# Tail operands of 128 columns, dilated casts in pieces of 1024 elements, and the last store on ScalarE's queue, in an attention + gated feed-forward kernel

## The chip, the cores and the metric

The kernel runs on one core of a Trainium2 chip. The metric is the device time of one execution in microseconds (us); the median of several executions counts. A core has five engines that run their own instruction streams: TensorE (PE; its weight loads are shown apart as PEld), VectorE (DVE), ScalarE (ACT), GpSimd (POOL) and SyncE (SP). DMA transfers are issued from the streams of SP, POOL or ACT, and all run on the same 16 DMA engines. The profile counts POOL's transfers under queue q0 and those of SP under q1.

## The reference

Inputs are q, k, v of 8 batches x 8 heads x 576 positions x 64, and the weights of a feed-forward part. Heads 0 to 3 look at a plain window of 32 positions back, heads 4 to 7 at every fourth position up to 128 back:

```python
mask_plain = (rel >= 0) & (rel < window)                                  # window = 32
mask_dil = (rel >= 0) & (rel < window * dilation) & (rel % dilation == 0)  # dilation = 4
scores = np.where(masks[None, :, :, :], scale * q @ k.T, -1000000000.0)
attn = softmax(scores)            # over the last axis
x = (attn @ v).transpose(0, 2, 1, 3).reshape(B * S, H * D)    # 4608 x 512
h = x @ w_in                      # 512 -> 2048
out = (h / (1 + exp(-beta * h))) @ w_out                       # 2048 -> 512, fp32
```

## The kernel before

**Two parts in one stream.** The attention of a batch produces 576 columns of xT, the transposed input of the feed-forward part. That part walks over 9 tiles of 512 tokens: for each tile 16 slots of `w_in` (L809, four matmuls of 512 columns, then tanh on ACT, L818, and the gate on DVE, L823) and 4 blocks of `w_out` (L844, sixteen matmuls, an eviction on ACT or DVE, L859 or L861, and a store from SP, L863). A planner (`Plan.run`) simulates all engines with estimated costs and writes every engine's instructions in the order in which it would start them, so that matmuls of the attention stand between those of the feed-forward part. This order is fixed when the program is built, as is the order of each DMA queue.

**Dilated heads.** Their 576 positions are four residues (position mod 4) of 144. In one residue the mask is a plain window of 32, so 128 of the 144 positions make one square of 128 x 128 (scores at L637, values at L712) and the last 16 positions, the *tail*, need the last 48 keys. Tail scores (task T, L607): for each head pair one matmul with `dkt` as stationary operand, 48 keys x 2 residues = 96 columns, and the 64 columns of `qt` moving, into 96 partitions of a bank. The exponential on ACT and a mask multiplication put the result into `ptt` (L574, L578). Tail values (task U, L697): eight matmuls a batch, stationary a slice of `ptt` with 96 rows and 64 columns, moving 65 columns of `vt_`, into 64 partitions. Each of the tasks runs once a batch, eight times in all. The plain heads' scores and values are L671 and L727. L637 and L671 use halves of 64 rows.

**How a batch comes in.** Batches 0 to 2 are loaded directly and transposed on TensorE (L446, L453). For batches 3 to 7, POOL casts q and k from float32 in HBM to bfloat16 in a scratch tensor in HBM, and SP transposes the scratch into SBUF with a DMA (`crossbar`, L436: dk and dq for the dilated heads, kT and qT for the plain ones). POOL's order for a batch is: a tiny `pace` copy (L921) that waits for the xT of the batch two earlier, the dilated cast of k, that of q, the plain cast of k, loads of v (st, two vt), the plain cast of q, another load of v (vp). A dilated cast is a copy of one contiguous stretch of 147,456 elements; the program before cuts it into 16 rows of 9216 elements. A plain cast moves runs of 64 elements.

**How a batch goes out.** From batch 2 on, normalized values go to a scratch tensor x in HBM (`back_dma`: x<-xsp L473, x<-xdm L481, x<-xdt L486) and SP transposes them into xT (L500). All of these, the crossbars of a later batch and the output stores stand in one queue order of SP: what waits there holds up everything issued behind it.

**The end.** The last block of 128 tokens is cut into columns 0 to 256, 256 to 384 and 384 to 512, each with its eviction and its store.

Of the kernel before, what the change touches and what calls it, by code (L numbers as in the profile page):

```python
# [9 lines left out]
BF16 = mybir.dt.bfloat16  # L10
ACT = mybir.ActivationFunctionType
# [163 lines left out]
def kernel(  # L175
# [19 lines left out]
    C = 4  # L195
    CT = S // C
    UT = CT - P
    KTL = UT + WIN
# [23 lines left out]
    const = lambda shape, dt, name: const_pool.tile(shape, dt, name=name)  # L222
    BANKS = [psum_pool.tile([P, 512], FP32, name=f"bank{i}") for i in range(8)]
    plan = Plan(range(8))
    E = {"ACT": nc.scalar, "DVE": nc.vector, "POOL": nc.gpsimd}

    def bank(g, dt=FP32):
        b = BANKS[g.bank][:]
        return b if dt == FP32 else b.bitcast(BF16)

    def copy(e, out, in_):
        (nc.scalar.copy if e == "ACT" else E[e].tensor_copy)(out=out, in_=in_)  # L232
# [21 lines left out]
    rcp = [const([P, 3, 2], FP32, f"rcp{i}") for i in range(8)]  # L254
    pt = [const([P, NI * 2, P], BF16, f"pt{x}") for x in range(2)]
    ptd = const([P, 2, 2, 4, P], BF16, "ptd")
    ptt = const([P, 2, 272], BF16, "ptt")
    ptt_own = ptt[0:2 * KTL, :, 0:256].rearrange("p c (m s) -> p c m s", s=2 * UT)[:, :, :, 0:UT]
    ptt_of = lambda c, h4: ptt[0:2 * KTL].rearrange("p c m -> p (c m)")[
        :, 256 * c + 64 * h4:256 * c + 64 * h4 + 64]  # L260
    xsp = [const([QT, 3, 2, 2, D], BF16, f"xsp{j}") for j in range(2)]
    xdm = const([P, C, 2, 2, D], BF16, "xdm")
    xdt = const([C * UT, 2, 2, D], BF16, "xdt")
# [9 lines left out]
    qt = [const([P, 2, 2, 4, UT], BF16, f"qt{i}") for i in range(2)]  # L273
    dk = [const([P, 2, 4, CT], BF16, f"dk{i}") for i in range(2)]
    dq = [const([P, 2, 4, CT], BF16, f"dq{i}") for i in range(2)]
    dkt = [const([P, 4, KTL, 2], BF16, f"dkt{i}") for i in range(2)]
    vp = [const([P, 4 * NI, DV], BF16, f"vp{i}") for i in range(2)]
    vd = [const([P, 4, C, DV], BF16, f"vd{i}") for i in range(2)]
    vt_ = [const([2 * KTL, 2, 4, DV], BF16, f"vt{i}") for i in range(2)]
# [3 lines left out]
    mm = lambda n: n / 2.4 + 2.5  # L283
# [16 lines left out]
    def t_fill1(e):  # L300
        for x in range(2):
            nc.vector.memset(kT[x][:, :, 0:WIN], 0.0)
            nc.vector.memset(qt[x][:], 0.0)
    fill1 = plan.op([("DVE", 300)], t_fill1, vt=-8)

    def t_fill2(e):
# [112 lines left out]
    def cast(b, z, h0, deps, vt):  # L419

        dst = scratch[b, z, h0] = dram_pool.tile([S * 4 * D], BF16, name=f"s{b}_{z}_{h0}")
        src = (k, q)[z][b, h0:h0 + 4]
        if h0:
            args = (dst[:].rearrange("(a e) -> a e", e=1024), src.rearrange("h s d -> (h s d)").rearrange("(a e) -> a e", e=1024))
        else:
            args = (dst[:].rearrange("(s h d) -> s h d", h=4, d=D), src.rearrange("h s d -> s h d"))
        return load("POOL", args, deps, vt, 576, .38 if h0 else .2, 500 if h0 else 1700)
# [76 lines left out]
    def attention(b, ld, names, vts):  # L504
# [3 lines left out]
        kv = b % 2  # L508
        if b < DIRECT:
            for n in [x for x in names if x[0] in "KQ"]:  # L510
                z, kind, i = "KQ".index(n[0]), n[1], int(n[2])
                vt = vt_of[n]
                g = Group("a")
                src = ld["qk", z, 0 if kind == "P" else 4]
                tr = plan.op([("PE", (18 * mm(64) if kind == "P" else 6 * mm(QT)))],
                             lambda e, g=g, z=z, kind=kind, i=i: t_transposes(g, z, kind, i),
# [15 lines left out]


        def mixed(e):
            copy(e, dkt[kv][:], dk[kv][:, :, :, CT - KTL:].rearrange("p r h k -> p h k r"))
        o = plan.op([("DVE", 450), ("POOL", 550)], mixed,
                    (steps["KD0"] + steps["KD1"] if b < DIRECT else ready["D"][0:1]) + war(("dkt", kv)), vt_of["T"] - .01, sbuf=True)
        used(("dk", kv, 0), o)
# [60 lines left out]
        for name in [n for n in names if n[0] in "ST"]:  # L599
            vt = vt_of[name]  # L600
            if name == "T":
                g = Group("s")

                def score(e, g=g):
                    sc = bank(g)[0:2 * KTL, 0:256].rearrange("p (c h r u) -> p h c r u", h=4, c=2, r=2)
                    for h4 in range(4):
                        nc.tensor.matmul(sc[:, h4], lhsT=dkt[kv][:, h4].rearrange("p k r -> p (k r)"),  # L607
                                         rhs=qt[kv][:, :, :, h4], start=True, stop=True)
                deps = tail_ready
                sop = plan.op([("PE", 4 * mm(64))], score,  # L610
                              deps, vt, acquire=g)
                used(("dkt", kv), sop)
                used(("qt", kv), sop)
                exp_and_mask(("T",), sop, g, vt, 256,
                             lambda g=g: bank(g)[0:2 * KTL, 0:256].rearrange("p (c m u) -> p c m u", c=2, u=UT),
                             lambda: ptt_own,
                             lambda: mask_t[0:2 * KTL].rearrange("p c h r u -> p c (h r) u"), [("pt", "T")])
                continue
            x = int(name[1])
# [69 lines left out]
        for name in [n for n in names if n[0] in "VU"]:  # L689
            vt = vt_of[name]  # L690
            g = Group("a")
            if name == "U":
                def values(e, g=g):
                    pv = bank(g)[0:C * UT, 0:4 * (D + 1)].rearrange("p (h e) -> p h e", h=4)
                    for h4 in range(4):
                        for c in range(2):
                            nc.tensor.matmul(pv[:, h4], lhsT=ptt_of(c, h4), rhs=vt_[kv][:, c, h4, 0:D + 1],  # L697
                                             start=(c == 0), stop=(c == 1))
                vop = plan.op([("PE", 8 * mm(D + 1))], values, [sdone["T",]] + vdeps["T"], vt, acquire=g)
                used(("vt", kv), vop)  # L700
                used(("pt", "T"), vop)
                normed("U", vop, g, vt, C * UT, 4,
                       lambda g=g: bank(g)[0:C * UT, 0:4 * (D + 1)].rearrange("p (h e) -> p h e", h=4),
                       xdt[:].rearrange("p x h d -> p (x h) d"), "xdt")
                continue
            x, j = int(name[1]), int(name[2])
            if x >= 2:
                def values(e, x=x, j=j, g=g):
                    pv = bank(g)[:, 0:4 * (D + 1)].rearrange("p (r h e) -> p r h e", r=2, h=2)
                    for r in range(2):  # L710
                        for a in range(2):
                            nc.tensor.matmul(pv[:, r, a], lhsT=ptd[:, x - 2, j, 2 * r + a],  # L712
                                             rhs=vd[kv][:, 2 * (x - 2) + a, 2 * r + j, 0:D + 1],
                                             start=True, stop=True)
                vop = plan.op([("PE", 4 * mm(D + 1))], values, [sdone[x, j]] + vdeps["D"], vt, acquire=g)
                used(("vd", kv), vop)
                used(("pt", x, j), vop)
                normed((x, j), vop, g, vt, P, 4,
                       lambda g=g: bank(g)[:, 0:4 * (D + 1)].rearrange("p (r h e) -> p r h e", r=2, h=2),
                       xdm[:].rearrange("p (r c) x h d -> p c r x h d", c=2)[:, j, :, x - 2], "xdm")  # L720
                continue

            def values(e, x=x, j=j, g=g):
                pv = bank(g)[:, 0:6 * (D + 1)].rearrange("p (m h e) -> p m h e", m=3, h=2)
                for a in range(3):
                    for h2 in range(2):
                        nc.tensor.matmul(pv[:, a, h2, :], lhsT=pt[x][:, (3 * j + a) * 2 + h2],  # L727
                                         rhs=vp[kv][:, (2 * x + h2) * NI + 3 * j + a, 0:D + 1],
                                         start=True, stop=True)
            vop = plan.op([("PE", 6 * mm(D + 1))], values,  # L730
                          [sdone[x, j, 0], sdone[x, j, 1]]
                          + vdeps["P", x], vt, acquire=g)
            used(("vp", kv), vop)
            for i in range(3 * j, 3 * j + 3):
                used(("pt", x, i), vop)
            normed((x, j), vop, g, vt, QT, 6,
                   lambda g=g: bank(g)[0:QT, 0:6 * (D + 1)].rearrange("p (m h e) -> p m h e", m=3, h=2),
                   xsp[j][:, :, x], ("xs", x, j))
# [3 lines left out]
        for name in [n for n in names if n[0] in "XY" and b < BY_DMA]:  # L742
            vt = vt_of[name]
            x = int(name[1])
            g = Group("a")
# [86 lines left out]
    def block(t, tb, vts):  # L832
        last_one = (t, tb) == (NTT - 1, 3)
        cuts = (0, HD // 2, 3 * HD // 4, HD) if last_one else (0, HD)
        for i, (lo, hi) in enumerate(zip(cuts, cuts[1:])):
            block_cols(t, tb, [x + i for x in vts], lo, hi)

    def block_cols(t, tb, vts, lo, hi):
        g = Group("z" if t == NTT - 1 else "o")
        prev = None  # L840
        for part in range(4):
# [15 lines left out]
        def evac(e):  # L857
            if e == "ACT":
                nc.scalar.mul(out=ob[:, lo:hi], in_=bank(g)[:, lo:hi], mul=0.5)  # L859
            else:  # L860
                nc.vector.tensor_single_scalar(out=ob[:, lo:hi], in_=bank(g)[:, lo:hi], scalar=0.5, op=ALU.mult)  # L861
        ev = plan.op([act(hi - lo), dve(hi - lo)], evac, [prev] + w, vts[3] - .01, group=g)
        so = plan.op([("SP", 400)], lambda e: nc.sync.dma_start(out=out[r0:r0 + P, lo:hi], in_=ob[:, lo:hi]),  # L863
                     [ev], vts[3], dma=.5 * (hi - lo) * 1000 / 350)
        used(key, so)

# [122 lines left out]
```

The softmax here doesn't subtract the row's maximum and nothing guards it: scores larger than these inputs give would overflow.

## Time and profile before

| what | value |
|---|---|
| device time, median of 5 executions | 308.0 us (307.39, 307.79, 308.0, 308.46, 309.72) |
| the profiled execution: own time / span from first to last instruction | 309.72 us / 308.0 us |
| TensorE clock granted | full in all 40 slices |
| L844 matmuls, 512 columns wide x560 | 140.6 us busy, 379 ns each with the drain |
| L809 matmuls, 512 columns wide x568 | 139.6 us busy, 379 ns each with the drain |
| L697 matmuls x64 / L607 matmuls x32 | 3.7 us, 198 ns each / 2.7 us, 206 ns each |
| DMA, mean 138 GB/s | 42.47 MB in 116,096 packets |
| q0 (POOL) / q1 (SP), share of the 16 engines' span | 62.6% / 37.0% |
| casts s<-in_k, s<-in_q, issue to landing, median | 7.4 us / 10.6 us |

Engines overlap, so busy times do not add up to the span. A matmul's shown duration includes its drain, which overlaps the next one; four matmuls of 512 columns stand 0.86 us apart from the next four. In an order of time, "[2.07 <-DMA x]" is idle time of the engine before that row and what ended it. In rows on DMA queues the columns are packets, MB written, and the packets' time as a share of 16 engines over the stretch asked for; packets of both queues can be under way in one engine at once, so that a share may pass 100%.

### The profile page before, as it was taken

What the parts mean: (1) busy time and instruction counts of PE and PEld (TensorE: products, weight loads), DVE (VectorE), ACT (ScalarE), POOL (GpSimd) and SP (SyncE); (2) the same over time, 40 slices, a digit from 0 to 9 for tenths busy, and PEclk for the clock granted to TensorE, in tenths of its full rate; (3) what the DMA queues carried; (4) which work ended last, traced back from release to release, by engine and by line L of the source; (5) the groups of instructions that cost most, each with busy time, mean ns of one, the idle gap of its engine ahead of it and who ended that gap; (6) DMA issues with size and microseconds to landing.
All of it is one profiled execution on the core that took longest, in us unless ns stands there. A gap on an engine that the chain in (4) does not pass through costs nothing.

```text
span 308.0 us, 6034 instructions
## 1 busy us (share of the span) xinstructions
PE 298.2 (97%) x2312; PEld 150.1 (49%) x2312; DVE 182.4 (59%) x420; ACT 170.8 (55%) x315; POOL 89.7 (29%) x132
## 2 busy tenths in 40 slices
PE   7899999999999979999999999999999999999995
PEld 5564545654544435445444444444444444444454
DVE  3578864988867645875677567756763434344300
ACT  2666963977447543765565556555555444455411
POOL 8987562845063106310641072200000000000000
PEclk9999999999999999999999999999999999999999
DMA  6999999999899999999899989995233100010122
GB/s 96 174 210 203 206 182 213 187 144 185 177 193 173 157 182 159 157 161 215 160 154 179 187 165 152 164 150 155 84 99 75 38 34 34 34 36 34 49 85 72
DMA packets 116096, 42.47 MB, mean 138 GB/s; under 512 B 93748, under 2 KB 110916, under 8 KB 115908
## 3 DMA queue, kind: packets, MB, share of 16 engines
q0 software_dynamic: 65392, 19.66, 62.6%
q1 hardware_dynamic: 50676, 22.43, 37.0%
q8 instruction: 18, 0.29, 0.4%
q14 instruction: 10, 0.08, 0.1%
HBM read 39.32 MB, written 18.87 MB: 189 GB/s over the span
## 4 chain that ended last, share of the span: by engine, by line
PE 74%; DMA 17%; DVE 4%; issue 1%; POOL 1%; SPq 1%; ACT 1%; POOLq 0%; ACTq 0%; DVEq 0%
PE bank L844 33%; PE bank L809 33%; DMA vd<-in_v_dram 4%; DMA st<-in_v_dram 4%; DMA xT<-x 3%; DMA dq<-s 3%; DMA st<-in_q_dram 2%; DVE g L823 2%; PE bank L727 1%; DMA x<-xsp 1%; PE bank L671 1%; PE bank L453 1%; PE bank L637 1%; PE bank L712 1%; PE bank L697 1%
## 5 line engine op out<-in xcount | busy, mean ns | idle before, releaser
L844 PE MATMUL bank<-w_out_bf,g 128*128 128x512 bf16 (+2 forms) x608 | 143.6, 368 | 0.0
L823 DVE SCALAR_TENSOR_TENSOR g<-tnh,bank 128x512 bf16<-128x512 bf16 x144 | 97.7, 684 | 75.0 <-ACT tnh L818 74.3
L809 PE MATMUL bank<-xT,w_in_bf 128*128 128x512 bf16 (+1 forms) x584 | 141.4, 376 | 0.5 <-DMA xT<-x 0.5
L818 ACT ACTIVATE tnh<-bank,beta_half 128x512 bf16<-128x512 f32 x144 | 98.5, 689 | 75.9 <-PE bank L809 74.8
L809 PEld LDWEIGHTS <-w_in_bf 128*128 128x128 bf16 x584 | 54.6, 98 | 60.8 <-DMA xT<-x 0.9
L844 PEld LDWEIGHTS <-g 128*128 128x128 bf16 x608 | 54.7, 98 | 55.8
L859 ACT ACTIVATE osb<-bank 128x512 f32<-128x512 f32 (+1 forms) x36 | 21.2, 589 | 32.2 <-PE bank L844 32.1
L574 ACT ACTIVATE pt<-bank 128x288 bf16<-128x288 f32 x64 | 21.6, 422 | 5.8 <-PE bank L671 5.8
L574 ACT ACTIVATE ptd<-bank 128x512 bf16<-128x512 f32 x32 | 16.9, 607 | 7.4 <-PE bank L637 7.4
L594 DVE TENSOR_TENSOR xsp<-bank,rcp 96x384 bf16<-96x384 f32 x32 | 17.7, 554 | 1.1
L382 POOL DMA_DIRECT2D vp<-in_v_dram x10 | 18.0, 1804 | 0.5 <-PE bank L453 0.5
L593 DVE RECIPROCAL rcp<-bank 128x4 f32<-128x4 f32 (+2 forms) x72 | 12.9, 179 | 6.8 <-PE bank L727 4.8
L578 DVE TENSOR_TENSOR ptd<-ptd,mask_d 128x512 bf16<-128x512 bf16 x27 | 11.9, 452 | 5.7 <-ACT ptd L574 4.5
L594 DVE TENSOR_TENSOR xdm<-bank,rcp 128x256 bf16<-128x256 f32 x32 | 13.6, 424 | 1.1
L382 POOL DMA_DIRECT2D vt<-in_v_dram x16 | 13.7, 1038 | 0.0
L382 POOL DMA_DIRECT2D s<-in_q_dram x10 | 13.6, 1356 | 0.0
L921 POOL COPY pace<-xT 1x2 bf16<-1x2 bf16 x4 | 0.7, 176 | 42.8 <-DMA xT<-x 35.7
L727 PEld LDWEIGHTS <-pt 128*128 128x128 bf16 x192 | 9.4, 97 | 5.9
L382 POOL DMA_DIRECT2D s<-in_k_dram x10 | 11.0, 1104 | 1.2 <-issue 1.2
L232 POOL COPY vd<-st 128x1024 bf16<-128x1024 bf16 x4 | 4.1, 1036 | 22.7 <-DMA st<-in_v_dram 22.7
L232 POOL COPY dkt<-dk 128x384 bf16<-128x384 bf16 x7 | 3.8, 541 | 23.8 <-DMA dk<-s 18.2
L727 PE MATMUL bank<-vp,pt 128*128 128x65 bf16 x192 | 10.4, 193 | 0.0
(107 smaller groups left out, 181.9 us busy)
## 6 DMA issues: line engine op xcount, KB each, us to landing
out_dram<-osb SPq DMA_DIRECT2D x35, 256.0 KB, 2.8
s<-in_k_dram POOLq DMA_DIRECT2D x10, 288.0 KB, 7.4
s<-in_q_dram POOLq DMA_DIRECT2D x10, 288.0 KB, 10.6
vp<-in_v_dram POOLq DMA_DIRECT2D x7, 384.0 KB, 18.5
w_out_bf<-in_moe_w_out_dram POOLq DMA_DIRECT2D x2, 1024.0 KB, 16.8
st<-in_k_dram POOLq DMA_DIRECT2D x6, 288.0 KB, 14.0
st<-in_q_dram POOLq DMA_DIRECT2D x6, 288.0 KB, 12.9
x<-xsp SPq DMA_DIRECT2D x12, 144.0 KB, 8.3
```

Source lines behind the costliest of these rows:

```text
L232: (nc.scalar.copy if e == "ACT" else E[e].tensor_copy)(out=out, in_=in_)
L382: {"POOL": nc.gpsimd, "SP": nc.sync}[queue].dma_start(out=out, in_=in_)
L574: nc.scalar.activation(out=w(), in_=sc(), func=ACT.Exp, scale=SCALE)
L578: E[e].tensor_tensor(out=w(), in0=w(), in1=m(), op=ALU.mult)
L593: nc.vector.reciprocal(out=r, in_=p[..., D])
L594: nc.vector.tensor_tensor(out=dst, in0=p[..., 0:D], in1=r.unsqueeze(len(p.shape) - 1).to_broadcast(list(p.shape[:-1]) + [D]), op=ALU.mult)
L727: nc.tensor.matmul(pv[:, a, h2, :], lhsT=pt[x][:, (3 * j + a) * 2 + h2], rhs=vp[kv][:, (2 * x + h2) * NI + 3 * j + a, 0:D + 1], start=True ...
L809: nc.tensor.matmul(bank(g)[:, a:z], lhsT=w_in_bf[:, kt, fb * P:(fb + 1) * P], rhs=xT[:, kt, xo + a:xo + z], start=(i == 0 and kt == kts[0] ...
L818: nc.scalar.activation(out=th[:, 0:n], in_=bank(g)[:, 0:n], func=ACT.Tanh, scale=beta_half[:, fb:fb + 1])
L823: nc.vector.scalar_tensor_tensor(out=g_t[t % 2][:, fb, c0:c0 + n], in0=th[:, 0:n], scalar=1.0, in1=bank(g)[:, 0:n], op0=ALU.add, op1=ALU.mult)
L844: nc.tensor.matmul(bank(g)[:, lo:hi], lhsT=g_t[t % 2][:, fb, tb * P:(tb + 1) * P], rhs=w_out_bf[:, fb, lo:hi], start=(fb == 0), stop=(fb = ...
L859: nc.scalar.mul(out=ob[:, lo:hi], in_=bank(g)[:, lo:hi], mul=0.5)
```

## The change

Three edits:

- **Tail.** `dkt` gets 32 more columns, zeroed at the start, and each tail score matmul takes 128 stationary columns from the start of its head's 96, so that the last 32 are those of the next head (or the zeros). It writes all 128 partitions of the bank; the exponential reads the first 96 as before. `ptt` is laid out flat with 32 more columns, and each tail value matmul takes 128 stationary columns instead of 64, the later 64 of the next slice; its result fills 128 partitions, of which the first 64 are read as before. The planner's cost of a tail score matmul goes from that of 64 columns to that of 68.
- **Dilated casts.** The same elements are copied in a view of 16 x 9 x 1024: the outer index takes every sixteenth piece of 1024 elements, and each outer entry has 9 such pieces, which are not contiguous.
- **Last store.** The store of the last 128 columns is issued from ACT instead of SP.

The order of the instructions on every engine is the same as before but for three points: DVE has two more memsets at the start, SP loses its last store, and ACT has it at its end.

```diff
-    ptt = const([P, 2, 272], BF16, "ptt")
-    ptt_own = ptt[0:2 * KTL, :, 0:256].rearrange("p c (m s) -> p c m s", s=2 * UT)[:, :, :, 0:UT]
-    ptt_of = lambda c, h4: ptt[0:2 * KTL].rearrange("p c m -> p (c m)")[
-        :, 256 * c + 64 * h4:256 * c + 64 * h4 + 64]
+    ptt = const([P, 2 * 272 + 32], BF16, "ptt")
+    ptt_own = ptt[0:2 * KTL, 0:2 * 272].rearrange("p (c m) -> p c m", c=2)[:, :, 0:256].rearrange(
+        "p c (m s) -> p c m s", s=2 * UT)[:, :, :, 0:UT]
+    ptt_of = lambda c, h4: ptt[0:2 * KTL, 256 * c + 64 * h4:256 * c + 64 * h4 + P]
...
-    dkt = [const([P, 4, KTL, 2], BF16, f"dkt{i}") for i in range(2)]
+    dkt_all = [const([P, 4 * 2 * KTL + 32], BF16, f"dkt{i}") for i in range(2)]
+    dkt = [d[:, 0:4 * 2 * KTL].rearrange("p (h k r) -> p h k r", h=4, r=2) for d in dkt_all]
...
             nc.vector.memset(qt[x][:], 0.0)
+            nc.vector.memset(dkt_all[x][:, 4 * 2 * KTL:], 0.0)
...
         if h0:
-            args = (dst[:].rearrange("(a e) -> a e", e=1024), src.rearrange("h s d -> (h s d)").rearrange("(a e) -> a e", e=1024))
+            args = [x.rearrange("(a c e) -> c a e", c=16, e=1024) for x in (dst[:], src.rearrange("h s d -> (h s d)"))]
...
-                    sc = bank(g)[0:2 * KTL, 0:256].rearrange("p (c h r u) -> p h c r u", h=4, c=2, r=2)
+                    sc = bank(g)[:, 0:256].rearrange("p (c h r u) -> p h c r u", h=4, c=2, r=2)
                     for h4 in range(4):
-                        nc.tensor.matmul(sc[:, h4], lhsT=dkt[kv][:, h4].rearrange("p k r -> p (k r)"),
+                        nc.tensor.matmul(sc[:, h4], lhsT=dkt_all[kv][:, 2 * KTL * h4:2 * KTL * h4 + P],
                                          rhs=qt[kv][:, :, :, h4], start=True, stop=True)
-                sop = plan.op([("PE", 4 * mm(64))], score,
+                sop = plan.op([("PE", 4 * mm(68))], score,
...
                 def values(e, g=g):
-                    pv = bank(g)[0:C * UT, 0:4 * (D + 1)].rearrange("p (h e) -> p h e", h=4)
+                    pv = bank(g)[:, 0:4 * (D + 1)].rearrange("p (h e) -> p h e", h=4)
...
-        so = plan.op([("SP", 400)], lambda e: nc.sync.dma_start(out=out[r0:r0 + P, lo:hi], in_=ob[:, lo:hi]),
+        so = plan.op([("ACT" if last_one and hi == HD else "SP", 400)],
+                     lambda e: (nc.scalar if e == "ACT" else nc.sync).dma_start(out=out[r0:r0 + P, lo:hi], in_=ob[:, lo:hi]),
                      [ev], vts[3], dma=.5 * (hi - lo) * 1000 / 350)
```

More of the change, by code (lines that the diff above doesn't have):

```diff
@@ L534, in mixed @@
         def mixed(e):
-            copy(e, dkt[kv][:], dk[kv][:, :, :, CT - KTL:].rearrange("p r h k -> p h k r"))
+            copy(e, dkt[kv], dk[kv][:, :, :, CT - KTL:].rearrange("p r h k -> p h k r"))
         o = plan.op([("DVE", 450), ("POOL", 550)], mixed,
@@ L835, in block, with block_cols @@
         for i, (lo, hi) in enumerate(zip(cuts, cuts[1:])):
-            block_cols(t, tb, [x + i for x in vts], lo, hi)
-    def block_cols(t, tb, vts, lo, hi):
+            block_cols(t, tb, [x + i for x in vts], lo, hi, last_one)
+    def block_cols(t, tb, vts, lo, hi, last_one):
         g = Group("z" if t == NTT - 1 else "o")
```

## The prediction

> **What bounds the kernel now.** I read the page first, then the groups of TensorE by shape, then its waits and its order of time, then the order of time of SP's queue, last the DMA queues in short windows. The page says that TensorE is the bound and that its own work leaves few holes:
>
> ```profile
> PE 298.2 (97%) x2312; PEld 150.1 (49%) x2312; DVE 182.4 (59%) x420; ACT 170.8 (55%) x315; POOL 89.7 (29%) x132
> PE 74%; DMA 17%; DVE 4%; issue 1%; POOL 1%; SPq 1%; ACT 1%; POOLq 0%; ACTq 0%; DVEq 0%
> ```
>
> 308.0 - 298.2 = 9.8 us are idle: some 4 before 45 us (first loads), 3.3 after the last matmul, and two waits for a transfer between. So two things shorten the time: TensorE's own work after 45 us, and those waits. This is TensorE's order of time at them, and around the tail of one batch:
>
> ```profile
> 112.18 0.62 PE L637 MATMUL bank<-dq,dk 64*128 64x128 bf16 x16 [2.07 <-DMA dq<-s]
> 113.61 0.33 PE L607 MATMUL bank<-qt,dkt 128*96 128x64 bf16 x4
> 113.77 1.03 PE L844 MATMUL bank<-w_out_bf,g 128*128 128x512 bf16 x4
> 114.63 0.28 PE L712 MATMUL bank<-vd,ptd 128*128 128x65 bf16 x4
> 114.76 1.03 PE L844 MATMUL bank<-w_out_bf,g 128*128 128x512 bf16 x4
> 115.62 0.41 PE L712 MATMUL bank<-vd,ptd 128*128 128x65 bf16 x8
> 115.86 1.02 PE L844 MATMUL bank<-w_out_bf,g 128*128 128x512 bf16 x4
> 116.73 0.29 PE L712 MATMUL bank<-vd,ptd 128*128 128x65 bf16 x4
> 116.94 0.44 PE L697 MATMUL bank<-vt,ptt 96*64 96x65 bf16 x8
> 117.31 1.04 PE L844 MATMUL bank<-w_out_bf,g 128*128 128x512 bf16 x4
> 209.79 1.47 PE L809 MATMUL bank<-xT,w_in_bf 128*128 128x512 bf16 x6 [0.45 <-DMA xT<-x]
> ```
>
> Columns: start, duration with the drain, then the work. What a group costs TensorE is the distance from its start to the next one's.
>
> **Part 1, the tail's wider stationary operands.** Nothing is added on TensorE: the same matmuls stream the same 64 or 65 columns and only the stationary side is wider. Tail values (L697, 8 matmuls): 117.31 - 116.94 = 0.37 us, where eight full-width L712 with the same 65 columns take 115.86 - 115.62 = 0.24. Entering them costs too: four L712 take 0.13 us (114.76 - 114.63) ahead of L844, but 0.21 (116.94 - 116.73) ahead of L697. So a tail costs 0.13 + 0.08 = 0.21 us more than full-width matmuls would. Tail scores (L607, 4 matmuls): 113.77 - 113.61 = 0.16 against 0.13, so 0.03. That 96 rows stay (L697) should not matter: L446 has 96*128 and shows neither an entry nor an exit cost, about 43 ns each for 96 columns.
>
> Behind the first 45 us there are seven L697 groups (at 49, 66, 83, 117, 147, 178 and 214 us) and six L607 groups (61, 80, 114, 144, 175, 206): 7 x 0.21 + 6 x 0.03 = 1.65 us; 3 x 0.21 + 2 x 0.03 = 0.69 of it lies ahead of the wait at 109.7 to 112.2, 0.96 behind. The earlier tails lie between waits for first loads and give nothing. Lower end nil (the width isn't the cause), upper end 2 us with the early ones. I take 1.65. It costs DVE two short memsets (the 128x16 ones took 65 to 85 ns) and a longer one in the first microseconds, where DVE waits for loads; on the path they would be 0.2 us.
>
> The Trainium skill has two rules here that disagree. "TensorE: Matmul & The Clock Gate", section "LDWEIGHTS (loading the stationary operand)", has the load take columns / 1.2 ns: 53 ns for 64 columns, 107 for 128, which speaks against the change; if all of it showed, 64 loads would lose 3.4 us and 32 loads from 80 to 107 ns another 0.9. Its section "Weight-path perf modes" has a fast load that needs all 128 columns. The rows side with the second:
>
> ```profile
> L697 PEld LDWEIGHTS <-ptt 96*64 96x64 bf16 x64 | 2.7, 110 | 1.7 <-DMA vt<-in_v_dram 0.8 <-issue 0.6
> L607 PEld LDWEIGHTS <-dkt 128*96 128x96 bf16 x32 | 2.5, 124 | 1.4
> L712 PEld LDWEIGHTS <-ptd 128*128 128x128 bf16 x128 | 6.7, 98 | 4.7 <-issue 0.2
> ```
>
> A full 128-column load takes 98 ns, one of 96 columns 124, one of 64 columns 110.
>
> **Part 2, the casts in pieces.** Each of batches 3 to 7 issues two dilated casts from POOL at its start. SP's queue while batch 4 is fetched:
>
> ```profile
> 88.56 0.63 SPq L473 DMA_DIRECT2D x<-xsp  x1
> 92.45 0.34 SPq L863 DMA_DIRECT2D out_dram<-osb  x1
> 97.92 1.52 SPq L500 DMA_TRANSPOSE xT<-x  x1
> 99.62 4.46 SPq L436 DMA_TRANSPOSE dk<-s  x1
> 104.14 2.72 SPq L436 DMA_TRANSPOSE dq<-s  x1
> ```
>
> SP waits from 92.8 to 97.9 for the x<-xsp issued at 88.56; all behind it (dk, then dq, which ends TensorE's 2.07 us) waits too. The casts were complete at 94.89 and 96.46, so SP was held by the store, not by them. Why 9.3 us, where the one issued at 77.51 took 4.2? The DMA queues from 119.5 to 121.5 us, 88.5 to 91 (two lines) and 102.5 to 106.5 (two lines):
>
> ```profile
> q0 software_dynamic: 16, 0.29, 123.9%
> ...
> q0 software_dynamic: 15, 0.28, 89.9%
> q1 hardware_dynamic: 57, 0.03, 4.7%
> ...
> q1 hardware_dynamic: 1679, 0.42, 81.6%
> q0 software_dynamic: 1630, 0.21, 78.9%
> ```
>
> A cast is 16 packets of 18 KB, one an engine, 1.4 to 3 us each; while they run SP's queue (q1) moves nearly nothing. With small packets in both queues they alternate one for one (1679 and 1630). In 2 KB pieces, 9 an engine and cast, SP's packets go between them. Ahead of and in x<-xsp stand 8 packets an engine of an output store (256 KB in 2 KB packets) and 18 of its own (288 rows of 512 B). The price of a piece is in no row for a copy from HBM to HBM. Nearest below: from 18.6 to 22.6 us q0 alone wrote 0.84 MB (505 packets, most of them 2 KB pieces of w_in), 210 GB/s, so the 0.59 MB of two casts take 2.8 us. Above: today's 0.59 MB from 119.5 to 124.8, 5.3 us. I take 4 us, 0.22 a piece. From 88.7, eight pieces pass with the output store (8 x (0.22 + 0.09) = 2.5, to 91.2), ten with x<-xsp (10 x (0.22 + 0.03) = 2.5, to 93.7), then eight of its packets against 32 ns ones (0.5, to 94.2), and some 0.8 us from last packet to landing as now: 95.0. SP goes on 2.9 us earlier, the casts land by then too (1.5 to 2 us earlier), and dq lands at 112.0 - 2.9 = 109.1, where TensorE wants it at 109.9 - 0.7 = 109.2. So the wait of 2.07 us just goes, and the 0.69 from ahead of it is kept. Ends: all 2.07 and no more; or nothing, when the pieces do not let q1 through.
>
> Against it speaks the Trainium skill, "DMA: Bandwidth & Descriptors", section "Queues, rings and completion order": an engine drains a whole packet, typically 9 to 17 descriptors, of one ring before it switches. If nine pieces are one such packet, nothing is won here; another section of the page, "SWDGE vs HWDGE vs iDMA", prefers packets of at most 4096 B, which is one or two pieces.
>
> Costs: each cast now has 144 rows instead of 16; POOL's issue took 0.51 to 0.57 us, loads of 192 to 256 rows (st) 0.64 to 0.78, so up to 0.25 each, 0.5 a batch ahead of the next issues on POOL. That is hidden: the plain cast issued at 88.49 sends its first packet at 93.5, behind the dilated ones in the ring. Uncovered, it is 0.5 us on the plain q cast, for which SP waits (196.9 to 202.2) before qT and the xT that TensorE awaits at 209.79. That wait of 0.45 I leave in: TensorE comes earlier, and so does the DMA side (casts of batch 5 wait for the xT of batch 3, behind the same SP queue). In batches 5 to 7 dq landed 5 to 6.7 us before L637 asked, so nothing more is to be gained there.
>
> **Part 3, the last store.** DVE ends the last eviction at 305.02; SP, busy until 305.19 with the store before, issues at 305.28 and sees it land at 306.90. ACT is free from 304.83, so it issues some 0.2 us earlier; SP's closing waits follow. Ends: a gain of 0.3, or a loss of 1 if a queue never used before starts slowly (stores from SP took 1.6 us at least and 2.7 at the median from issue to landing; no row shows one from ACT). Nothing stands behind it on ACT. I take -0.2.
>
> **Sum.** 1.65 + 2.07 + 0.2 = 3.9 us off the profiled execution's 309.72 (span 308.0 and 1.72 around it): 305.8. Of the runs shown it is the slowest, 1.7 over the median 308.0; TensorE's clock is full throughout, so what differs is probably waits, and I credit the median with two thirds of the 2.07 (1.4): 308.0 - 1.65 - 1.4 - 0.2 = 304.7.
>
> **Rivals.**
> *The casts' pieces free nothing* (0.20). For it: nothing shows how the two rings mix at 2 KB. The wait stays and swallows the 0.69; the wait at 209.79 swallows up to 0.75 of the 0.96, so 0.2 to 0.96 + 0.2: 306.8 to 307.6, say 307.2.
> *The width is not what L697 pays for* (0.06). The entry cost would then stay because of its 96 rows; L446 speaks against. 308.0 - 1.4 - 0.2 = 306.4.
> *The pieces slow the casting queue* (0.13). Place: q0's ring, each piece now waiting for a q1 packet; the plain q cast of batch 7 lands after 202.2 - (what TensorE gains), SP issues qT and xT late, and L809 at 209.79 has no slack. Price: at 0.33 us a piece (3 us, the longest packet, over 9) two casts take 6 us and the mixing adds 1, so 1.7 more a batch; three batches (5 to 7) follow one another through POOL's pace copy, 5.1 in all, less 1.65 + 0.2 gained: 311; with one or two batches passing it on 309 to 310. I give it 309.8. It decides from a slip of 0.7 us a batch. Against it: SP's backlog of 290 to 600 packets, now drained after the casts at the cost of the plain ones, goes in their shadow.
>
> **Numbers.** Forecast 304.7 (0.61), own range 302.9 to 306.2. An 8-in-10 range takes in most of the first rival: 302.9 to 308.0. What this kernel's runs can tell from no change is about 0.5%, 1.5 us: faster is under 306.5, slower over 309.5. Faster 0.59 of the forecast's, 0.04 of the width's, 0.05 of the first rival's: 0.68; slower 0.11, from the third; same 0.21.
>
> **What would show it.** L697 with 128 columns: eight in 0.24 us, loads of 98 ns, no 0.08 ahead of them. Right after the casts start, q1 with hundreds of packets where it has 57; x<-xsp of batch 2 landed by about 95, dq issued before 102, L637 of batch 4 without a wait, or one under 0.7. Wrong if the wait at L637 stays at 2 us, if SP's wait for the plain casts (202.2) or L809's 0.45 grow beyond 1 us, or if the last store lands over 1.7 us after its issue.

## The result and the profile after

| kernel | median of its executions, us | lowest to highest | ratio to before, 95% interval |
|---|---|---|---|
| before | 307.68 (56 executions, the five of the table above among them) | 306.41 to 310.85 | |
| after | 305.76 (30 executions) | 304.98 to 307.2 | 0.994 (0.9927 to 0.9953) |

The change saves 1.9 us, 0.6%; the interval of the ratio is 1.45 to 2.25 us of 307.68. The forecast was a gain of 3.3. The profiled execution of after took 306.6 us with a span of 304.9, 3.1 us less than the one shown of before. That is more than the medians differ, so the two traces cannot simply be subtracted. What of it is the change, and what is one execution against another, is the main question below.

This is the page of after: span, busy times, the two DMA queues, ACT's new queue q10 (packets, MB, share of the 16 engines) and the chain by engine:

```profile
span 304.9 us, 6036 instructions
PE 296.5 (97%) x2312; PEld 149.1 (49%) x2312; DVE 182.1 (60%) x422; ACT 170.9 (56%) x315; POOL 90.3 (30%) x132
q0 software_dynamic: 66672, 19.66, 63.7%
q1 hardware_dynamic: 50532, 22.36, 36.5%
q10 hardware_dynamic: 144, 0.07, 0.1%
PE 72%; DMA 18%; DVE 4%; ACT 2%; issue 1%; POOL 1%; SPq 1%; POOLq 0%; ACTq 0%; DVEq 0%
```

TensorE is still the bound and has 1.7 us less to do (298.2 before). The DMA share of the chain did not fall. TensorE's order of time in after, at the wait for batch 4 and around the next tail, answers to the rows of before:

```profile
110.96 0.62 PE L639 MATMUL bank<-dq,dk 64*128 64x128 bf16 x16 [1.43 <-DMA dq<-s]
...
112.39 0.28 PE L609 MATMUL bank<-qt,dkt 128*128 128x64 bf16 x4
112.50 1.03 PE L846 MATMUL bank<-w_out_bf,g 128*128 128x512 bf16 x4
...
114.36 0.41 PE L714 MATMUL bank<-vd,ptd 128*128 128x65 bf16 x8
114.60 1.02 PE L846 MATMUL bank<-w_out_bf,g 128*128 128x512 bf16 x4
115.46 0.28 PE L714 MATMUL bank<-vd,ptd 128*128 128x65 bf16 x4
115.58 0.41 PE L699 MATMUL bank<-vt,ptt 96*128 96x65 bf16 x8
115.83 1.03 PE L846 MATMUL bank<-w_out_bf,g 128*128 128x512 bf16 x4
```

The lines stand two or three further down than in before: L639 was L637, L609 was L607, L699 was L697, L714 was L712, L846 was L844, and the store L866 was L863. Below, a line is called by its number in the kernel it is read in.

The tail now costs what full-width matmuls cost. From start to start, eight tail values take 115.83 - 115.58 = 0.25 us (0.37 before), the four L714 ahead of them 0.12 (0.21 before), four tail scores 112.50 - 112.39 = 0.11 (0.16 before). That is 0.21 and 0.05 a batch. The weight loads show it as well (groups by shape; the pair is busy time and mean ns of one):

```profile
L699 PEld LDWEIGHTS <-ptt 96*128 96x128 bf16 x64 | 2.6, 97 | 1.4 <-DMA vt<-in_v_dram 1.0 <-issue 0.2
L609 PEld LDWEIGHTS <-dkt 128*128 128x128 bf16 x32 | 1.9, 98 | 1.5
```

They fell from 110 and 124 ns to 97 and 98, although L699 still has 96 rows.

But the wait at L639 is there: 1.43 us where 2.07 stood and nothing to 0.7 was forecast. SP's order of time in after, over the same stretch as before:

```profile
88.55 1.69 SPq L475 DMA_DIRECT2D x<-xsp  x1
91.88 0.34 SPq L866 DMA_DIRECT2D out_dram<-osb  x1
96.12 1.56 SPq L502 DMA_TRANSPOSE xT<-x  x1
97.86 4.12 SPq L438 DMA_TRANSPOSE dk<-s  x1
102.03 2.82 SPq L438 DMA_TRANSPOSE dq<-s  x1
```

SP goes on at 96.12 instead of 97.92 and issues dq at 102.03 instead of 104.14. So SP's store gets through sooner, though not by the 2.9 us forecast. Of these 2.1 us at the issue only 1.2 are left at the landing: dq landed at 110.82 in after and at 112.04 in before. The DMA queues show SP's packets passing in the five microseconds from 88.5, first in before, then in after (packets, MB, share of the 16 engines):

```profile
q0 software_dynamic: 46, 0.57, 84.7%
q1 hardware_dynamic: 152, 0.21, 12.3%
```

```profile
q0 software_dynamic: 254, 0.49, 73.7%
q1 hardware_dynamic: 264, 0.32, 20.5%
```

Where the pieces meet the output store that stands ahead of x<-xsp, they pass one for one. In after, from 90.25 to 91.5 us:

```profile
q0 software_dynamic: 75, 0.15, 73.9%
q1 hardware_dynamic: 75, 0.15, 36.2%
```

Last the end, DVE's last eviction and the store issued from ACT, in order of time:

```profile
301.77 0.29 DVE L863 TENSOR_SCALAR osb<-bank 128x128 f32<-128x128 f32 x1 [1.30 <-PE bank L846]
302.15 0.38 ACTq L866 DMA_DIRECT2D out_dram<-osb  x1
```

The issue comes 0.09 us after the eviction's end (0.26 before), and the store lands at 303.77, 1.62 us after its issue.

### The profile page after: what moved, and what is told of

Same layout as the page of the kernel before. It is cut to its first block, busy times and chain, and to the rows that moved or that the text cites. A ratio compares the mean times of both kernels' runs of the same rounds, so it can differ in the third digit from the quotient of the medians.

```text
span 304.9 us, 6036 instructions
## 1 busy us (share of the span) xinstructions
PE 296.5 (97%) x2312; PEld 149.1 (49%) x2312; DVE 182.1 (60%) x422; ACT 170.9 (56%) x315; POOL 90.3 (30%) x132
## 4 chain that ended last, share of the span: by engine, by line
PE 72%; DMA 18%; DVE 4%; ACT 2%; issue 1%; POOL 1%; SPq 1%; POOLq 0%; ACTq 0%; DVEq 0%
PE bank L846 33%; PE bank L811 32%; DMA vd<-in_v_dram 4%; DMA st<-in_q_dram 4%; DMA st<-in_v_dram 3%; DMA dq<-s 3%; DVE g L825 2%; DMA st<-in_k_dram 2%; DMA x<-xsp 2%; DMA xT<-x 1%; PE bank L729 1%; PE bank L673 1%; PE bank L639 1%; PE bank L714 1%; ACT ptd L576 1%
## 5 line engine op out<-in xcount | busy, mean ns | idle before, releaser
L846 PE MATMUL bank<-w_out_bf,g 128*128 128x512 bf16 (+2 forms) x608 | 143.3, 368 | 0.0
L846 PEld LDWEIGHTS <-g 128*128 128x128 bf16 x608 | 54.6, 98 | 55.7
L576 ACT ACTIVATE ptd<-bank 128x512 bf16<-128x512 f32 x32 | 16.9, 603 | 6.8 <-PE bank L639 6.7
L232 POOL COPY vd<-st 128x1024 bf16<-128x1024 bf16 x4 | 4.1, 1036 | 16.3 <-DMA st<-in_v_dram 16.3
## 6 DMA issues: line engine op xcount, KB each, us to landing
w_out_bf<-in_moe_w_out_dram POOLq DMA_DIRECT2D x2, 1024.0 KB, 16.7
```

What stands on the lines that cost most here:

```text
L576: nc.scalar.activation(out=w(), in_=sc(), func=ACT.Exp, scale=SCALE)
L846: nc.tensor.matmul(bank(g)[:, lo:hi], lhsT=g_t[t % 2][:, fb, tb * P:(tb + 1) * P], rhs=w_out_bf[:, fb, lo:hi], start=(fb == 0), stop=(fb = ...
```

## The experiments

Theory: SP's store, held up behind large cast packets, was what made dq late, and pieces cure it. Rival: the DMA engines are full from the casts until dq lands, so that the order of the packets hardly matters, only their number. Where a table says "cast to dq", it is the time from the issue of batch 4's dilated k cast to the landing of its dq, in the one profiled execution. Each kernel is compared with executions of before measured beside it, through the ratio; it is formed from the executions and is not exactly the quotient of the two medians.

### One part at a time

Tail alone: the kernel before with the tail edit, without these two:

```diff
-            args = [x.rearrange("(a c e) -> c a e", c=16, e=1024) for x in (dst[:], src.rearrange("h s d -> (h s d)"))]
+            args = (dst[:].rearrange("(a e) -> a e", e=1024), src.rearrange("h s d -> (h s d)").rearrange("(a e) -> a e", e=1024))
...
-        so = plan.op([("ACT" if last_one and hi == HD else "SP", 400)],
+        so = plan.op([("SP", 400)],
```

> The kernel before with the tail's edit alone. Waits theory (the wait of L637 for dq of batch 4 and that of L809 for xT swallow what TensorE gains ahead of them): the eight L697 take 0.24 us and four L607 0.12, yet of the 1.65 us only the part behind the waits stays, 0.2 to 1.1 us: 306.6 to 307.5 against 307.7; the wait at L637 grows to 2.5 to 2.9 us in the profile. Rival (in most executions these waits are short, so TensorE's work is the bound): the whole 1.65 stays, 306.0.

The casts alone, with the first of these two lines as in after and the other edits undone:

> The kernel before with the dilated casts in pieces alone. Waits theory: x<-xsp of batch 2 lands 1.5 to 2.5 us earlier after the casts' start, dq of batch 4 lands 1 to 2 us earlier, L637 waits 0.5 to 1.2 us in place of 2.07 and the 0.45 of L809 goes: 306.2 to 306.9 against 307.7. Rival (the waits are short in most executions): no change within 0.3 us.

The store alone, with only the second line as in after:

> The kernel before with the last store on ACT's queue alone. Both theories: issue 0.1 to 0.2 us after DVE's last eviction and landing 1.6 us later, 0.15 to 0.2 us less from the last matmul to the end: 307.5. Rival: the closing waits of SP end at the same time, 307.7.

| kernel | median, us | before beside it | ratio, 95% | cast to dq, us | wait for dq, us |
|---|---|---|---|---|---|
| tail alone | 306.0 | 307.49 | 0.994 (0.9912 to 0.9968) | 24.61 | 1.77 |
| casts alone | 306.89 | 307.49 | 0.9972 (0.9944 to 0.9999) | 23.85 | 0.39 |
| last store alone | 307.36 | 307.49 | 0.9989 (0.9962 to 1.0016) | 24.60 | 2.08 |

The tail alone has the ratio of the whole change. Its order of time, with the wait and the group of tail values:

```profile
110.61 0.62 PE L639 MATMUL bank<-dq,dk 64*128 64x128 bf16 x16 [1.77 <-DMA dq<-s]
...
115.23 0.41 PE L699 MATMUL bank<-vt,ptt 96*128 96x65 bf16 x8
115.47 1.03 PE L846 MATMUL bank<-w_out_bf,g 128*128 128x512 bf16 x4
```

The wait stays near its old length and yet the kernel is 1.5 us faster by the medians, 1.8 by the ratio (1.0 to 2.7). What the waits theory expected the waits to take back of the tail's gain (a wait of 2.5 to 2.9 us and 306.6 to 307.5), they did not take back; the number that came is its rival's, 306.0.

The casts alone bring 0.2% to 0.3%, at the limit of what can be told. The last store alone cannot be told from nothing in the time, but the trace shows it:

```profile
306.53 0.29 DVE L861 TENSOR_SCALAR osb<-bank 128x128 f32<-128x128 f32 x1 [1.30 <-PE bank L844]
306.90 0.38 ACTq L864 DMA_DIRECT2D out_dram<-osb  x1
```

The issue again stands 0.08 us behind the eviction, and from the start of the last matmul to the end of the span it takes 3.37 us, as in after, where before and the tail alone have 3.54 and 3.53. So 0.17 us. (TensorE ran at half rate from 114 to 117 us in this profiled execution, mean granted clock 0.993, so its span of 309.6 is not used.)

### Another execution of before

> The kernel before, looked at once more. Corrected theory: its wait at L637 differs from one execution to the next with the start of batch 4's casts; 1.4 to 2.3 us, cast to dq 23.5 to 24.7. Rival (it is nearly always 2.07): 1.9 to 2.2 and 24.5 to 24.7.

Another profiled execution of before took 306.61 us with a span of 304.9. TensorE's order of time:

```profile
106.79 2.75 PE L844 MATMUL bank<-w_out_bf,g 128*128 128x512 bf16 x12
109.47 0.62 PE L637 MATMUL bank<-dq,dk 64*128 64x128 bf16 x16
```

No wait stands between these rows. The 2.07 us on which the forecast rested 1.4 of its 3.3 belong to the slow end of before's executions: cast to dq took 23.22 us here and 24.61 there. Both the expectation (a wait of 1.4 to 2.3 us) and its rival missed. The wait for xT of 0.45 us at 209.79 is missing here, too, so that its absence from after's trace is not to be put down to the change. Nor are SP's clock times. Its order of time here, with the old rows:

```profile
96.36 1.87 SPq L500 DMA_TRANSPOSE xT<-x  x1
98.41 3.93 SPq L436 DMA_TRANSPOSE dk<-s  x1
102.38 2.72 SPq L436 DMA_TRANSPOSE dq<-s  x1
```

These are nearly the times of after (96.12 and 102.03), because the casts were issued at 86.06 us here, at 87.43 in the first execution and at 87.80 in after. Only times counted from the casts can be compared: SP goes on 10.5 and 10.3 us after them in the two executions of before, 8.3 in after.

With two executions of before, the span can be cut at the wait, at the start of the matmuls that need dq of batch 4:

| execution | span | start of L637/L639 | from there to the end |
|---|---|---|---|
| before, first | 308.0 | 112.18 | 195.8 (with the 0.45 wait for xT) |
| before, second | 304.9 | 109.47 | 195.4 |
| casts alone | 304.5 | 109.31 | 195.2 |
| tail alone | 304.7 | 110.61 | 194.1 |
| after | 304.9 | 110.96 | 193.9 |

The right column scatters little and shows the change: 195.2 to 194.1 is the tail's width (1.1 us; four batches at 0.21 + 0.05 make 1.04) and 194.1 to 193.9 the store. Executions that differ in the casts alone are still up to 0.2 us apart here (195.4 and 195.2) without a wait that the traces show. The middle column scatters by 2.7 us within one kernel and shows nothing of the change. Set against the medians, with some 1.7 us around the span: before's median puts the start of L637 at 307.68 - 1.7 - 195.4 (or 195.8) = 110.6 (or 110.2), after's at 305.76 - 1.7 - 193.9 = 110.2. Between nothing and 0.4 us of the 1.9 was won ahead of this point, with 0.4 either way for the ratio's interval; the forecast had 0.69 + 1.4 = 2.1 there.

### Are pieces what frees SP, and does their size matter?

After with its casts in the old rows, and with pieces of 512 and of 3072 elements:

```diff
-            args = [x.rearrange("(a c e) -> c a e", c=16, e=1024) for x in (dst[:], src.rearrange("h s d -> (h s d)"))]
+            args = (dst[:].rearrange("(a e) -> a e", e=1024), src.rearrange("h s d -> (h s d)").rearrange("(a e) -> a e", e=1024))
...
+            args = [x.rearrange("(a c e) -> c a e", c=16, e=512) for x in (dst[:], src.rearrange("h s d -> (h s d)"))]
...
+            args = [x.rearrange("(a c e) -> c a e", c=16, e=3072) for x in (dst[:], src.rearrange("h s d -> (h s d)"))]
```

> The changed kernel with the casts back in 16 rows of 9216 elements. Corrected theory (the wait of L637 runs from TensorE's own work on batch 2, some 35 us earlier, so tails ahead of that are not swallowed, and the pieces shorten the way from the cast's issue to dq of batch 4 from 24.6 to some 23 us): 306.0 to 306.4, 0.2 to 0.6 over the changed kernel's 305.8; cast to dq 24.5 to 24.7, L637 waits 1.8 to 2.2 us. Rival (the pieces bring nothing to the time): 305.7 to 305.9.

> The changed kernel with pieces of 512 elements, 18 an engine and cast. Mixing theory (SP's packets go between the pieces, one for one): the output store and x<-xsp of batch 2 pass sooner, cast to dq of batch 4 22 to 22.7 us, 305.2 to 305.6. Rival (SP's transfers start some 4 us after their issue under load, whatever the piece): cast to dq 23 to 23.8 as with 1024, 305.6 to 306.0.

> The changed kernel with pieces of 3072 elements, 3 an engine and cast. Mixing theory: with 6 pieces an engine for both casts only 6 of the 26 packets of SP pass during them, cast to dq 24 to 24.5 us, L637 waits 1.5 to 2 us, 306.0 to 306.4. Rival (any cut does): cast to dq 23 to 23.8, 305.7.

| casts of after in | median, us | ratio to before, 95% | cast to dq, us | wait for dq, us |
|---|---|---|---|---|
| 16 rows of 9216 | 305.94 | 0.9956 (0.9929 to 0.9983) | 23.61 | 1.01 |
| pieces of 3072 | 306.16 | 0.9964 (0.995 to 0.9977) | 23.70 | 1.04 |
| pieces of 1024 (after) | 305.76 | 0.994 (0.9927 to 0.9953) | 23.02 | 1.43 |
| pieces of 512 | 306.1 | 0.9948 (0.993 to 0.9966) | 23.03 | 0.48 |

The four intervals overlap; once the tail is wide, the pieces cannot be told from nothing. The theories of the pieces missed with all three sizes: the old rows did not bring cast to dq back to 24.5 us, nor did it fall to 22.7 with pieces of 512 or rise to 24 with pieces of 3072.

Over all kernels here that leave the other transfers of this stretch alone (some come further down), the time from the issue of x<-xsp to that of xT, which waits for its landing, was 8.1 to 9.4 us in six executions with the old rows and 6.6 to 7.7 in four with pieces of 1024. So the pieces do free SP, by 1.3 us on average. Cast to dq took 24.61, 24.61, 24.60, 24.46, 23.61 and 23.22 us with the old rows (mean 24.2) and 23.02, 23.85, 23.34 and 24.05 with pieces of 1024 (mean 23.6). That is 0.6 us, and the spread of either set is larger.

### Does it help to free SP altogether?

In after, eight output stores that stand in SP's queue around the casts (token tiles 1 and 2) are issued from ACT:

```diff
-                     lambda e: (nc.scalar if e == "ACT" else nc.sync).dma_start(out=out[r0:r0 + P, lo:hi], in_=ob[:, lo:hi]),
+                     lambda e: (nc.scalar if e == "ACT" or t in (1, 2) else nc.sync).dma_start(out=out[r0:r0 + P, lo:hi], in_=ob[:, lo:hi]),
```

> The changed kernel, with the eight output stores of token tiles 1 and 2 issued from ACT in the place of its order where the planner had put SP's issue after the eviction; no other instruction moves. It takes the output stores out of SP's queue ahead of x<-xsp of batch 2. Theory that x<-xsp stands behind the 8 store packets an engine: x<-xsp lands 1.5 to 2.5 us earlier, cast to dq of batch 4 21 to 22 us, L637 without a wait, 304.8 to 305.2. Rival (x<-xsp starts 4 us after its issue under load whatever stands ahead): cast to dq 22.8 to 23.6, 305.6 to 306; ACT's issues (0.38 us each) may add 0.2.

The median was 305.82, ratio 0.9964 (0.9941 to 0.9988), where the theory of the stores had 304.8 to 305.2. The profile is of the slowest of the twelve executions (308.87 us), so its waits are not those of the median. SP's order of time, then TensorE's wait and a new one 30 us later:

```profile
86.78 0.35 SPq L475 DMA_DIRECT2D x<-xsp  x1
90.94 3.36 SPq L502 DMA_TRANSPOSE xT<-x  x1
95.28 4.19 SPq L438 DMA_TRANSPOSE dk<-s  x1
99.55 4.77 SPq L438 DMA_TRANSPOSE dq<-s  x1
```

```profile
111.31 0.62 PE L639 MATMUL bank<-dq,dk 64*128 64x128 bf16 x16 [2.88 <-DMA dq<-s]
...
142.22 1.02 PE L846 MATMUL bank<-w_out_bf,g 128*128 128x512 bf16 x4 [1.75 <-DVE g L825]
```

SP goes on at 90.94, five microseconds earlier than in after, and issues dq 2.5 us earlier, at 99.55. Yet dq lands at 111.18, 0.4 later than in after; counted from the casts it is 24.1 us, where the expectations had at most 23.6. So in this execution freeing SP did not bring dq earlier, and the median shows no gain either. (The wait of 1.75 at L846 is for DVE's gate; whether ACT's additional issues caused it is not shown.)

### Does it help to move less?

In after, the plain q cast of batch 4 is left out:

```diff
-                c = cast(b, z, h0, [go], b - 2 + .01 * n)
+                if (b, z, h0) == (4, 1, 0):
+                    scratch[b, z, h0] = scratch[b - 1, z, h0]
+                    c = plan.op([("POOL", 1700)], lambda e: None, [go], b - 2 + .01 * n, dma=576 * 1024 / .2 / 1000, lat=1100)
+                else:
+                    c = cast(b, z, h0, [go], b - 2 + .01 * n)
```

> The changed kernel without the plain cast of q of batch 4: its crossbar transposes the scratch of batch 3 instead, so that the plain heads of batch 4 get other queries. It takes 2304 of the some 9,100 to 9,400 packets of POOL's queue out of the stretch from the casts to dq of batch 4. Throughput theory (the engines are full in that stretch in every kernel, so dq lands when the packets of both queues are through, in whatever order): cast to dq of batch 4 falls from 23.0 to 19 to 21 us, L637 has no wait, 304.6 to 305.2. Rival (dq is held by the order of SP's queue and by transfers that start late): cast to dq 22.5 to 23.5, wait and time as in the changed kernel, 305.8.

Median 304.59, ratio 0.9894 (0.9868 to 0.9919), cast to dq 19.95 us. TensorE goes through without a wait:

```profile
106.20 2.75 PE L846 MATMUL bank<-w_out_bf,g 128*128 128x512 bf16 x12
108.88 0.62 PE L639 MATMUL bank<-dq,dk 64*128 64x128 bf16 x16
```

The throughput theory's numbers came. Its interval lies below after's, as no other kernel's does. SP issues dq late even so:

```profile
102.91 1.36 SPq L438 DMA_TRANSPOSE dq<-s  x1
```

| execution | dq issued, us after the casts | dq landed, us after the casts | from issue to landing, us |
|---|---|---|---|
| before, first | 16.7 | 24.61 | 7.9 |
| before, second | 16.3 | 23.22 | 6.9 |
| after | 14.2 | 23.02 | 8.8 |
| stores from ACT | 12.5 | 24.08 | 11.6 |
| without the plain q cast | 15.9 | 19.95 | 4.0 |

The earlier dq was issued, the longer it took to land, except where less was to be moved: there it was issued 1.7 us later than in after and landed 3.1 us earlier. That decides against SP's queue as what held dq.

The DMA queues from the first packet of the dilated casts to the landing of dq say why. First before (88.7 to 112.0 us), then after (89.0 to 110.8), then this kernel (88.2 to 106.9):

```profile
q0 software_dynamic: 9120, 1.93, 99.1%
q1 hardware_dynamic: 4939, 1.77, 53.9%
```

```profile
q0 software_dynamic: 9376, 1.93, 105.5%
q1 hardware_dynamic: 4945, 1.77, 51.5%
```

```profile
q0 software_dynamic: 7056, 1.64, 99.3%
q1 hardware_dynamic: 4909, 1.77, 46.7%
```

The shares sum to some 150% in all three, and in no microsecond after the first does the packets' time of both queues fall under 82% of the 16 engines. (A sum of over 100% does not mean that both queues run: from 99 to 102 us in before q0 has 235% and q1 not a packet.) Before dq lands, the same 9,100 to 9,400 packets of q0 and the same 4,900 of q1 have gone through in before and in after; the pieces change their order. With 2,320 packets and 0.29 MB fewer the same stretch is 3.1 us shorter. So it is bound by what must be moved; whether the packets or the bytes count is not separated here. Runs of 64 elements, 128 bytes written, make 8,448 of q0's 9,120 packets in before: 4,608 in the two plain casts, the others in loads of v.

### Does it help to start earlier?

The pace copy of batch 4 waits for both halves of an xT; here it reads only from the first half. The second kernel has, besides, the old rows of the casts:

```diff
-                    xT[0:1, 0, mid - 1:mid + 1] if b - 2 >= BY_DMA else g_t[b % 2][0:1, 0, 0:2]))
+                    xT[0:1, 0, mid - 1 - (b == 4):mid + 1 - (b == 4)] if b - 2 >= BY_DMA else g_t[b % 2][0:1, 0, 0:2]))
```

> The changed kernel, with the pace copy of batch 4 reading columns of the first half of xT of batch 2 alone, so that the casts of batch 4 wait for one transpose less and start 1.1 us earlier; nothing else is moved. Waits theory: dq of batch 4 lands some 1 us earlier and L637's wait falls from 1.4 to 0.3 to 0.6 us: 304.7 to 305.0 against 305.8 for the changed kernel. Rival (dq is held by the output store and x<-xsp in SP's queue, which do not move): 305.7 to 306.0 and the wait stays.

> The kernel of pace4 with the casts back in 16 rows of 9216 elements. Throughput theory: the pieces are worth about 1 us on the way to dq of batch 4, and the earlier casts already take the wait away, so L637 waits 0 to 0.9 us and the time is 305.1 to 305.7, within 0.5 of pace4. Rival (the pieces are worth their time elsewhere too): 305.8 to 306.3.

And the same for all of batches 4 to 7:

```diff
+                    xT[0:1, 0, mid - 2:mid] if b - 2 >= BY_DMA else g_t[b % 2][0:1, 0, 0:2]))
```

> The changed kernel with the pace copies of batches 4 to 7 all reading columns of the first half of xT of the batch two earlier alone. Throughput theory: batch 4 as with pace4 (no wait at L637); the casts of batches 5 to 7 start up to some us earlier, where L637 had 5 us to spare anyway, so nothing more is won, or up to 0.5 us lost to their running beside the transposes before: 305.0 to 305.6. Rival (earlier casts help everywhere): under 304.8.

| kernel | median, us | ratio to before, 95% | casts issued at, us | cast to dq, us | wait for dq, us |
|---|---|---|---|---|---|
| batch 4 earlier, pieces of 1024 | 305.14 | 0.9906 (0.9872 to 0.994) | 84.67 | 23.34 | none |
| batch 4 earlier, old rows | 305.39 | 0.9924 (0.9897 to 0.995) | 84.90 | 24.46 | 0.42 |
| batches 4 to 7 earlier, pieces | 312.45 (306.77 to 313.81) | no verdict | 84.98 | 24.05 | 0.85 |

With an earlier start of one batch's casts the wait is gone or 0.42 us, where the other kernels issued them at 85.3 to 87.8. That is one execution of each, and before's second one had no wait with casts at 86.06, so it is a hint only. The first time lies between its theory and its rival, the second in the range of its theory. The first of these has the best time of all kernels that compute the whole, but its interval reaches into after's, so that it is not shown to be faster. With all batches both expectations failed. The pace copies of batches 5 to 7 come 5 to 9 us earlier than in after, and TensorE has two waits for transfers that after does not have:

```profile
115.83 0.43 PE L673 MATMUL bank<-qT,kT 64*128 64x96 bf16 x12 [0.77 <-DMA qT<-s]
...
120.10 1.25 PE L811 MATMUL bank<-xT,w_in_bf 128*128 128x512 bf16 x5 [0.96 <-DMA xT<-x]
```

These are of the fastest execution (306.77). That the earlier casts of batch 5 crowd these transfers is likely but not shown. The other five took 311.7 to 313.8 us with a mean granted clock of 0.987 to 0.995; they left no profile, and what slowed them stays open.

## Why the prediction was right, and where not

**The direction and the range held; 304.7 was 1.1 us too low.** The sum was made of three terms, one of which was mis-sized: 1.4 us for the wait, where between nothing and 0.4 was won ahead of it. Some of the nearness is luck. The sum started from 308.0, the median of five executions, and 56 executions have 307.68; without these 0.3 us the miss would be 1.3. And 307.68 less the two terms that held, 1.65 and 0.2, is 305.8, so with the tail's whole term the measured 305.76 needs nothing from the wait.

**Tail: right.** The mechanism (the stationary side's width is what is paid for, at the group and at its entry) and the size held: 0.21 us for the values as forecast, 0.05 instead of 0.03 for the scores. Taken alone it gives 307.49 - 306.0 = 1.5 us by the medians, 1.8 by the ratio, where 1.65 was forecast. The 96 rows that stay cost nothing, as argued from L446, so the rival that named the rows fell. The Trainium skill's rule of columns / 1.2 ns ("TensorE: Matmul & The Clock Gate", section "LDWEIGHTS (loading the stationary operand)") does not hold for these loads: 128 columns took 97 ns where 64 took 110.

**Casts: the step "So the wait of 2.07 us just goes" failed.** It had two faults.
- Its size was taken from one execution, and from the slowest of the five shown. Crediting the median with two thirds of it (1.4) corrected this too little: another execution of the same program has no wait at all.
- It followed SP's queue and stopped at the issue. "SP goes on 2.9 us earlier" came true with 1.8 (2.2 counted from the casts), but the next step, that dq would land earlier by the same, took the time from issue to landing as fixed. It is not: dq issued 2.1 us earlier lands 1.2 us earlier, or (eight stores moved) 4.6 us earlier than in before and lands 0.9 us earlier, and with the plain q cast left out it took 4.0 us from issue to landing where after took 8.8. The engines are busy (82% or more) until dq has landed. Cast to dq fell by 0.6 us on average in place of 2.9.

The price of a piece was also low: 0.22 us was taken; the 18 pieces of each engine took from 89.1 to 95.3 us, 0.34 each with what passed between them. The mixing was half as forecast: the output store's packets passed one for one with the pieces, but the 512-byte packets of x<-xsp, forecast among the last ten pieces from 91.2 us, began at 93.5. The Trainium skill's statement on draining 9 to 17 descriptors of a ring before a switch ("DMA: Bandwidth & Descriptors", section "Queues, rings and completion order") could have made nine pieces one turn. The trace shows no sign of it: from 90.25 to 91.5 us 75 pieces and 75 packets of SP passed, though it does not name the engine of a packet.

**Waits that swallow: only half of the rival came true.** The rival "The casts' pieces free nothing" stood nearest in mechanism, but its 307.2 was too high: it let the wait at 209.79 swallow up to 0.75 us behind L637, and this wait was gone, in one execution of before as well. Behind L637 the tail's gain comes through entire (1.1 us). Ahead of it the whole change kept 0 to 0.4 of the 0.69 forecast, uncertain by 0.4; the tail alone kept 0.4 by its median and 0.7 by its ratio, uncertain by 0.9. The casts start after TensorE's work on batch 2, so a part of the gain there should move the wait's end, too; the scatter of single executions hides whether it does, and that stays open.

**Pieces that slow the casting queue** did not come: from the first cast's issue to the landing of the plain q cast it took 17.5 us in batch 4 in after, 19.35 and 16.9 in the two executions of before; in batch 7, where the rival had its place, 18.4 against 23.3 and 18.8. (The 3 us that it took for the longest packet was low: in batch 4 one took 3.3.)

**Last store: right**, 0.17 for 0.2. A queue used for the first time at the end of the kernel cost no start: 1.62 us to landing, against 1.62 from SP.

The saving of 1.9 us then is: 1.1 for the tail behind L637, 0.17 for the store, 0.2 to 0.6 behind L637 that scatters from execution to execution (0.45 of it the wait for xT), and what is left, 0 to 0.4, ahead of it. How much of this last part is the tail's and how much the pieces' stays open.

## What to carry to other kernels

Take a wait's length from more than one execution before spending it: one that a transfer ends can be 2 us in one execution and nothing in the next, and cutting the span at that wait separates what is steady (the work behind it) from what scatters. When a queue's head is blocked, ask first whether the DMA engines have spare time until the transfer that is awaited lands; if not, reordering the packets wins little, as here, and having less to move wins more. In matmuls with few moving columns, 128 stationary columns can be cheaper than 64, even if half the result is thrown away.

## What the runs showed of the hardware

- Entering a group of 64-column stationary operands cost 0.08 to 0.09 us on the matmuls ahead, beside 0.12 in the group itself (eight in 0.37 instead of 0.25). Four matmuls with 96 columns cost 0.05 more than with 128.
- Under full DMA engines a transfer from SP began late: xT, issued at 97.92 us in before, sent its first packet at 102.2; one issued at 224.12 with idle engines sent it at 225.45.
- A cast copy in rows of 9216 elements is 18 KB a packet and nearly shuts the other queue out for 1.4 to 3.3 us at a time; cut to 2 KB, the median piece took 0.17 us and one in ten 0.36 or more. That this moved the time so little is the study's main lesson, not a contradiction.
